# Two-pass inducing-point attention: the second pass three batches behind the first, with weights loaded in pieces

## The chip, the cores and the metric

One core of one Trainium2 chip runs the whole program. The metric is device time in microseconds (us), median over several executions; lower is better. The profile is of one execution; its span, from the first to the last recorded instruction, is about 2 us shorter than the time measured for the same execution (159.9 against 161.84 us for the kernel before).

Executions of this program differ by 1 to 3%, and the clock that is granted to the matmul engine differs between them. Runs are therefore marked fast or slow: a run of a single-core program counts as slow when it is over 1.5% above the fastest of its kernel.

Short names: PE is the matmul engine, DVE the vector engine, ACT the scalar (activation) engine, POOL the GpSimd engine. The names L148 and so on are lines of the kernel.

## The reference, cut to what matters

```python
# x: (4, 12480, 128) f32, inducing: (32, 128), w_in: (128, 2048), w_out: (2048, 128)
def mab(q, kv):
    s = scale * (q @ kv.transpose(0, 2, 1))
    a = np.exp(s - s.max(-1, keepdims=True))
    a /= a.sum(-1, keepdims=True) + 1e-09
    return a @ kv
h   = mab(I, x)        # 32 inducing points attend to all rows of a batch
att = mab(x, h)        # every row attends to the 32 points of its batch
g   = gelu(att @ w_in) # exact gelu
out = g @ w_out        # (49920, 128) f32
```

There are two passes over x. No row of a batch can enter the second pass before the whole batch has gone through the first, because `h` sums over all rows. The values are so small that the kernel takes the two-layer network on the 32 points instead of on every row: it works out q, 32 rows of 128, per batch, and the second pass averages rows of q. A check on the core tests the conditions of that shortcut and branches to a general version if they fail. They hold here.

## The kernel before: the parts that matter

A batch is cut into 7 units, 6 of 2048 rows and a tail of 192; there are 28 units in all. `s` is the step; a step does pieces of the first pass for the newest units and of the second pass for units that are LAG steps older:

```python
    LAG = n_u + 5                      # 12 units
    ...
        a0, a1, a2 = au(0), au(1), au(2)      # first pass: units s, s-1, s-2
        b0, b1 = bu(0), bu(1)                 # second pass: units s-LAG, s-LAG-1
        lone = a0 is None
        if a0: a_transpose(bat(a0), a0, 0)    # PE transposes x, DVE copies to xT
        if a1: a_score(bat(a1), a1)           # PE scores, ACT exponential e1t, POOL adds to acc
        if a0: load_next()                    # issues the DMA of a later unit of x
        pump()                                # one stage of precompute, if one is pending
        if b1:
            b_sum(bat(b1), b1)                # PE sums e2, DVE reciprocal
            b_out(bat(b1), b1, 0, False)      # PE matmul 'at', DVE scales it into o
            b_out(bat(b1), b1, 1, True)       # PE matmul 'at', ACT copies, POOL scales
        pump()
        if a0: a_transpose(bat(a0), a0, 1)
        if b0: b_score(bat(b0), b0)           # PE scores, ACT exponential e2 (2 buffers)
        pump()
        if b1:
            b_out(bat(b1), b1, 2, False)
            b_out(bat(b1), b1, 3, lone)       # the last one also issues the 1 MB output DMA
        pump()
        if a2:
            a_gather(bat(a2), a2)             # PE gathers e1t * x into hun
            if a2.tail: chains.append(precompute(bat(a2)))
```

`precompute` makes q of a batch after its tail: hT (the 32 points), pt = w_in applied to them (PE), slope and offs (DVE), then

```python
        nc.gpsimd.tensor_tensor(out=sl, in0=pt, in1=slope..., op=ALU.mult)      # POOL, 128x512
        nc.gpsimd.tensor_tensor(out=gl, in0=sl, in1=offs..., op=ALU.subtract)   # POOL, 128x512
        yield
        ... qp_ps += gl.T @ w_out_h  (16 matmuls on PE), then q
```

The loads of x come in as f16 into 9 buffers `xh`; an `xh` buffer comes free when its gather is done. Loads are issued from POOL's queue, outputs from SP's. The weights are loaded whole:

```python
    for _ in range(3): load_next()            # two were issued before: units 0 to 4
    nc.gpsimd.dma_start(out=w_in_h, in_=moe_w_in)
    nc.gpsimd.dma_start(out=w_out_h, in_=moe_w_out...)
    for _ in range(3): load_next()            # units 5 to 7
```

The order of instructions on an engine's queue is settled when the program is built, and it is not the order of the Python lines: in the trace below, PE does the scores of a unit ahead of the four `at` matmuls of an earlier one, two of which are written first. I call this the built order, and "in turn" the order of the lines.

Of the kernel before, what the change touches and what calls it, by code (L numbers as in the profile page):

```python
# [8 lines left out]
FP32 = mybir.dt.float32  # L9
FP16 = mybir.dt.float16  # L10
INT32 = mybir.dt.int32
AF = mybir.ActivationFunctionType
ALU = mybir.AluOpType
AX = mybir.AxisListType

B = 4
N = 12480
M = 32
C = 128
DFF = 2048  # L20
NBLK = DFF // 128
# [35 lines left out]
def kernel(  # L57
# [8 lines left out]
    nc = tc.nc  # L66
# [1 line left out]

    consts = ctx.enter_context(tc.tile_pool(name="consts", bufs=1))
    main = ExitStack()  # L70
    xt_pool = main.enter_context(tc.tile_pool(name="xt", bufs=3))
    sb = main.enter_context(tc.tile_pool(name="sb", bufs=2))
    pre = main.enter_context(tc.tile_pool(name="pre", bufs=2))
    ps = main.enter_context(tc.tile_pool(name="ps", bufs=1, space=PSUM))

    units = [[Unit(b, i) for i in range(NFULL + 1)] for b in range(B)]
# [24 lines left out]
    w_in_h = consts.tile([128, DFF], FP16)  # L101
    w_out_h = consts.tile([128, NBLK, 128], FP16)
# [3 lines left out]
    for j in range(4):  # L106
# [3 lines left out]
        out=stack4,  # L110
        in_=identity.rearrange("p (j m) -> p m j", j=4),
        axis=AX.X,
        op=ALU.add,
# [3 lines left out]
        out=same_m, in_=stack4.unsqueeze(1).broadcast_to([128, 4, M])  # L117
# [4 lines left out]
    n_u = NFULL + 1  # L122
# [4 lines left out]
    class Batch:  # L127
        def __init__(self, b):
            self.b = b
            self.rr2 = pre.tile([128, n_u, 4, 4], FP32, tag="rr2")  # L130
            nc.gpsimd.memset(self.rr2[:, NFULL, :, :], 1.0 / M)
            self.xT = xt_pool.tile([128, N], FP16, tag="xT", name=f"xT{b}")

            self.acc = pre.tile([128, 16, M], FP32, tag="acc")
            self.hun = ps.tile([128, C], FP32, tag="hun", name=f"hun{b}")
            self.live = {}

        def xT_of(self, u, c0, c1):
            return self.xT[:, u.t0 + c0 * u.p : u.t0 + c1 * u.p]
# [111 lines left out]
    def precompute(bt):  # L251
        hun_sb = pre.tile([128, C], FP32, tag="hun_sb")
        nc.scalar.activation(out=hun_sb, in_=bt.hun, func=AF.Copy)
        r1s = pre.tile([128, M], FP32, tag="r1s")
        nc.vector.tensor_reduce(
            out=r1s, in_=bt.acc.rearrange("p c m -> p m c"), axis=AX.X, op=ALU.add
        )
        yield
        h_ps = ps.tile([128, 2, M], FP32, tag="misc")
        nc.tensor.matmul(h_ps[:, 0, :], ones_f, r1s, start=True, stop=True)  # L260
        nc.tensor.matmul(h_ps[:, 1, :], hun_sb, stack4, start=True, stop=True)
        yield
        rr1 = pre.tile([128, M], FP32, tag="rr1")
        nc.vector.reciprocal(out=rr1, in_=h_ps[:, 0, :])
        in_range(rr1, 1.0 / R_HIGH, 1.0 / R1_LOW, bt.b, 0)
        bt.hT = pre.tile([128, M], FP16, tag="hT")
        nc.vector.tensor_tensor(out=bt.hT, in0=h_ps[:, 1, :], in1=rr1, op=ALU.mult)

        yield
        pt_ps = ps.tile([128, NBLK, M], FP32, tag="misc")  # L270
        for blk in range(NBLK):
            nc.tensor.matmul(
                pt_ps[:, blk, :],
                w_in_h[:, blk * 128 : (blk + 1) * 128],
                bt.hT,
                start=True,
                stop=True,
            )
        yield
        pt = pre.tile([128, NBLK, M], FP32, tag="pt")  # L280
        nc.scalar.activation(out=pt, in_=pt_ps, func=AF.Copy)
        hs = pre.tile([128, NBLK], FP32, tag="hs")
        nc.vector.tensor_reduce(out=hs, in_=pt, axis=AX.X, op=ALU.add)
        slope = pre.tile([128, NBLK], FP32, tag="slope")
        nc.vector.tensor_scalar(
            out=slope,
            in0=hs,
            scalar1=2.0 * CGELU / M,
            scalar2=0.5,
            op0=ALU.mult,  # L290
            op1=ALU.add,
        )
        offs = pre.tile([128, NBLK], FP32, tag="offs")
        nc.vector.scalar_tensor_tensor(
            out=offs,
            in0=hs,
            scalar=CGELU / (M * M),
            in1=hs,
            op0=ALU.mult,
            op1=ALU.mult,  # L300
        )
        sl = pre.tile([128, NBLK, M], FP32, tag="sl")
        nc.gpsimd.tensor_tensor(
            out=sl,
            in0=pt,
            in1=slope.unsqueeze(2).broadcast_to([128, NBLK, M]),
            op=ALU.mult,
        )
        gl = pre.tile([128, NBLK, M], FP16, tag="gl")
        nc.gpsimd.tensor_tensor(  # L310
            out=gl,
            in0=sl,
            in1=offs.unsqueeze(2).broadcast_to([128, NBLK, M]),
            op=ALU.subtract,
        )
        yield
        qp_ps = ps.tile([128, 128], FP32, tag="misc")
        for blk in range(NBLK):
            j = blk % 4
            nc.tensor.matmul(  # L320
                qp_ps[32 * j : 32 * j + 32, :],
                gl[:, blk, :],
                w_out_h[:, blk, :],
                start=(blk < 4),
                stop=(blk >= NBLK - 4),
            )
        yield
        qp = pre.tile([128, 128], FP32, tag="qp")
        nc.scalar.activation(out=qp, in_=qp_ps, func=AF.Copy)
        yield  # L330
        q_ps = ps.tile([128, 128], FP32, tag="misc")
        nc.tensor.matmul(q_ps, same_m.rearrange("p j m -> p (j m)"), qp, start=True, stop=True)
        bt.q = pre.tile([128, 4, 128], FP16, tag="q")
        nc.vector.tensor_tensor(  # L334
            out=bt.q,
            in0=q_ps.unsqueeze(1).broadcast_to([128, 4, 128]),
            in1=strand.unsqueeze(2).broadcast_to([128, 4, 128]),
            op=ALU.mult,
        )
        yield  # L340
        check_gelu(bt, pt, hs)
# [34 lines left out]
        o = sb.tile([128, 16, 128], FP32, tag="o", bufs=4)  # L376
        bt.live[("o", u.idx)] = o

    def b_out(bt, u, ci, on_act):
        if ci >= u.nci:  # L380
            return
        e2 = bt.live[("e2", u.idx)]
        o = bt.live[("o", u.idx)]
        rr2 = bt.rr2[:, u.idx, :, :]
        ov = o[:, : u.nc, :].rearrange("p (j ci) d -> p ci j d", ci=u.nci)
        at = ps.tile([128, 4, 128], FP32, tag="big", bufs=4)
        nc.tensor.matmul(  # L387
            at[: u.p, : u.nj, :],
            e2[: u.rows, ci * u.p : (ci + 1) * u.p],
            bt.q[: u.rows, : u.nj, :],  # L390
            start=True,
            stop=True,
        )
        dst = ov[: u.p, ci, :, :]
        by = rr2[: u.p, ci, : u.nj].unsqueeze(2).broadcast_to([u.p, u.nj, 128])
        if on_act:
            nc.scalar.activation(out=dst, in_=at[: u.p, : u.nj, :], func=AF.Copy)  # L397
            nc.gpsimd.tensor_tensor(out=dst, in0=dst, in1=by, op=ALU.mult)  # L398
        else:
            nc.vector.tensor_tensor(out=dst, in0=at[: u.p, : u.nj, :], in1=by, op=ALU.mult)  # L400
        if ci == u.nci - 1:
            base = u.b * N + u.t0
            nc.sync.dma_start(
                out=out[base : base + u.nc * u.p, :].rearrange(
                    "(p c) d -> p c d", p=u.p
                ),
                in_=o[: u.p, : u.nc, :],
            )

    order = [u for b in range(B) for u in units[b]]  # L410
# [2 lines left out]
    def load_next():  # L413
        nonlocal loaded
        if loaded < len(order):
            a_load(order[loaded])
            loaded += 1

    n_all = B * n_u

    LAG = n_u + 5
    batches = {}

    def at_step(s):
# [8 lines left out]
        def bat(u):  # L433
            if u.b not in batches:
                batches[u.b] = Batch(u.b)
            return batches[u.b]

        def pump():
            if chains:
                try:  # L440
                    next(chains[0])
                except StopIteration:
                    chains.pop(0)

        a0, a1, a2 = au(0), au(1), au(2)
        b0, b1 = bu(0), bu(1)
        lone = a0 is None
        if a0:
            a_transpose(bat(a0), a0, 0)
        if a1:  # L450
            a_score(bat(a1), a1)
        if a0:
            load_next()
        pump()
        if b1:
            b_sum(bat(b1), b1)
            b_out(bat(b1), b1, 0, False)
            b_out(bat(b1), b1, 1, True)
        pump()
        if a0:  # L460
            a_transpose(bat(a0), a0, 1)
# [1 line left out]
            b_score(bat(b0), b0)  # L463
        pump()
        if b1:
            b_out(bat(b1), b1, 2, False)
            b_out(bat(b1), b1, 3, lone)
        pump()
        if a2:
            a_gather(bat(a2), a2)  # L470
# [9 lines left out]
            )  # L480

    chains = []
    for _ in range(3):
        load_next()
    nc.gpsimd.dma_start(out=w_in_h, in_=moe_w_in)
    nc.gpsimd.dma_start(
        out=w_out_h, in_=moe_w_out.rearrange("(blk p) d -> p blk d", p=128)
    )
    for _ in range(3):
        load_next()  # L490
    for s in range(n_all + LAG + 1):
        at_step(s)

# [12 lines left out]
        out=failed,  # L506
        in0=tot,
# [177 lines left out]
```

## Time and profile before

| | before |
|---|---|
| time, four runs in all | 161.52 us median (160.19 to 162.86) |
| first and last output issued | 56.2 and 152.2 us |
| PE, POOL, DVE, ACT busy | 73%, 60%, 55%, 48% of the span |
| second pass alone at clock 0.5 | 3.39 us a unit |

(The profiled run took 161.84 us; it carries the slow mark, but it lies in the middle of the kernel's four runs.)

The slice rows of the page cut the span into 40 slices of 4 us. A digit is the busy share of a slice in tenths; PEclk is the granted clock of PE in tenths; GB/s is what the DMA engines moved. Of the kernel before:

```profile
PE   0379606987865999997699999599798568888400
...
PEclk9999955699998579999858999779999755556755
DMA  2999999999999899999999986506679835378991
GB/s 39 212 212 212 193 209 213 213 213 212 214 214 199 141 199 284 377 331 304 323 310 287 415 359 271 234 37 246 271 291 394 359 144 189 146 320 322 410 384 37
```

Two things are to be seen. Until about 50 us the DMA is full at 212 GB/s, counted in f16, with loads alone. And after 92 us the DMA is often not full although only outputs are left, which go at up to 410 GB/s in a slice. The Trainium skill ("Trainium Kernel Development and Optimization", Key Constraints) says that DMAs from all queues share the same 16 engines; the trace agrees, for from 60 to 92 us loads and outputs run together and the DMA row stays at 9.

The windows view gives busy time by stretch. Its columns are: from and to, length, busy us (and instructions) of PE, PEld, DVE, ACT and POOL, clock, DMA share, GB/s. Of the kernel before:

```profile
0.00:56.00 56.00, 35.98 (x664) 27.96 (x665) 17.95 (x45) 23.57 (x36) 31.75 (x51) 0.86 1.03 193
56.00:92.00 36.00, 33.12 (x501) 21.34 (x499) 30.67 (x73) 21.55 (x36) 23.04 (x31) 0.88 1.03 315
92.00:152.00 60.00, 47.41 (x489) 21.83 (x486) 40.06 (x113) 31.48 (x61) 40.46 (x46) 0.78 0.65 267
```

A share of 1.03 is to be read as full. The last stretch has a DMA share of 0.65 in 60 us: 60 x 0.35 = 21 us of empty DMA. The bytes to be moved are 13.8 MB in, 25.6 MB out, so empty DMA in the body of the program is the time that could be won.

Why the DMA runs empty there is in the chain of waits, followed back from the end; each line has start, length and what. Of the kernel before, one unit of second pass alone at clock 0.5:

```profile
134.53 0.61 ACT e_2539 L354
...
135.18 0.27 PE r_2549 L366 x4
135.46 0.55 PE s_2563 L346 x4
136.00 1.83 PE at L387 x4
...
137.92 0.61 ACT e_2568 L354
```

From one exponential to the next is 137.92 - 134.53 = 3.39 us. `at` of 136.00 belongs to the unit before e_2539. There are two e buffers, so the exponential e_2568 can only start when those four `at` matmuls have read the old buffer, and the sum of the next unit and the scores of the one after it go first.

### The profile page before, as it was taken

The page shows a single profiled execution, that of the slowest core. Times are in us where ns is not written, and L with a number is a line of the kernel's source. Part 1 is how long each engine was busy: PE and PEld are TensorE (multiplying, and loading weights), DVE is VectorE, ACT ScalarE, POOL GpSimd, SP SyncE. Part 2 cuts the span into 40 slices and gives each one's busy share as a digit, 9 for nine tenths or more (in the row PEclk, how much of TensorE's full clock was granted, in tenths as well). Part 3 has the DMA queues.
Part 4 walks back from the last instruction along what each step waited for, and adds up shares of the span by engine and source line. Part 5 has one row for each costly group of instructions (what it writes and reads, how often), then busy time and mean ns, then how long its engine had stood idle before and what let it go on. Part 6 is the DMA issues. An engine that isn't in the chain of part 4 may idle for free. (4 is left out here: it accounts for less than half of the span.)

```text
span 159.9 us, 4086 instructions
## 1 busy us (share of the span) xinstructions
PE 116.5 (73%) x1647; PEld 71.1 (44%) x1647; DVE 88.7 (55%) x229; ACT 76.6 (48%) x132; POOL 95.3 (60%) x127
## 2 busy tenths in 40 slices
PE   0379606987865999997699999599798568888400
PEld 0367406866753466666345757365323232223100
DVE  2223102223542998899859779588777772554700
ACT  3045601667373365684455667337666324446400
POOL 7823710564839963799673457835969950667900
PEclk9999955699998579999858999779999755556755
DMA  2999999999999899999999986506679835378991
GB/s 39 212 212 212 193 209 213 213 213 212 214 214 199 141 199 284 377 331 304 323 310 287 415 359 271 234 37 246 271 291 394 359 144 189 146 320 322 410 384 37
DMA packets 10087, 39.71 MB, mean 248 GB/s; under 512 B 2992, under 2 KB 3792, under 8 KB 6992
## 3 DMA queue, kind: packets, MB, share of 16 engines
q0 software_dynamic: 6112, 13.83, 46.3%
q1 hardware_dynamic: 3952, 25.58, 39.5%
q8 instruction: 14, 0.23, 0.5%
q14 instruction: 9, 0.07, 0.1%
HBM read 27.67 MB, written 25.56 MB: 333 GB/s over the span
## 5 line engine op out<-in xcount | busy, mean ns | idle before, releaser
L148 PE MATMUL tr<-identity_h,xh 128*128 128x128 f16 x392 | 36.3, 246 | 12.7 <-DMA xh<-in_x_dram 12.4
L148 PEld LDWEIGHTS <-xh 128*128 128x128 f16 x392 | 27.9, 111 | 21.2 <-DMA xh<-in_x_dram 14.3
L175 POOL TENSOR_TENSOR acc<-acc,e1t 128x512 f32<-128x512 f32 (+1 forms) x24 | 24.4, 1016 | 17.7 <-ACT e1t L168 15.5
L397 ACT ACTIVATE o<-at 128x512 f32<-128x512 f32 (+1 forms) x39 | 21.4, 562 | 12.6 <-PE at L387 8.1
L83 POOL DMA_DIRECT2D xh<-in_x_dram x28 | 15.9, 570 | 9.9 <-DMA xh<-in_x_dram 3.7
L398 POOL TENSOR_TENSOR o<-o,rr_1587 128x512 f32<-128x512 f32 (+1 forms) x13 | 12.5, 992 | 8.1 <-ACT o L397 8.1
L153 DVE COPY xT_118<-tr 128x1024 f16<-128x1024 f16 (+1 forms) x7 | 4.4, 629 | 19.1 <-PE tr L148 19.1
L155 ACT ACTIVATE xT_118<-tr 128x1024 f16<-128x1024 f16 x6 | 6.0, 1024 | 17.0 <-PE tr L148 17.0
L398 POOL TENSOR_TENSOR o<-o,rr_947 128x512 f32<-128x512 f32 (+1 forms) x12 | 11.7, 988 | 3.8 <-ACT o L397 2.3
L400 DVE TENSOR_TENSOR o<-at,rr_459 128x512 f32<-128x512 f32 (+1 forms) x19 | 11.9, 658 | 1.9 <-PE at L387 1.8
L400 DVE TENSOR_TENSOR o<-at,rr_116 128x512 f32<-128x512 f32 (+1 forms) x19 | 12.0, 658 | 0.3 <-PE at L387 0.2
L185 PEld LDWEIGHTS <-e1t 128*32 128x32 f16 x392 | 7.4, 98 | 6.7 <-issue 4.6
L153 DVE COPY xT_461<-tr 128x1024 f16<-128x1024 f16 (+1 forms) x7 | 4.4, 629 | 9.7 <-PE tr L148 9.7
L400 DVE TENSOR_TENSOR o<-at,rr_947 128x512 f32<-128x512 f32 (+1 forms) x14 | 8.8, 650 | 0.2
L155 ACT ACTIVATE xT_461<-tr 128x1024 f16<-128x1024 f16 x6 | 6.2, 1025 | 4.7 <-PE tr L148 4.7
L400 DVE TENSOR_TENSOR o<-at,rr_1587 128x512 f32<-128x512 f32 (+1 forms) x13 | 7.7, 639 | 0.0
L398 POOL TENSOR_TENSOR o<-o,rr_459 128x512 f32<-128x512 f32 (+1 forms) x7 | 6.6, 949 | 1.7 <-ACT o L397 1.7
L346 PEld LDWEIGHTS <-hT 128*32 128x32 f16 x100 | 4.0, 97 | 7.3 <-issue 6.1
L155 ACT ACTIVATE xT_949<-tr 128x1024 f16<-128x1024 f16 x6 | 6.2, 1027 | 1.9 <-PE tr L148 1.8
L155 ACT ACTIVATE xT_1589<-tr 128x1024 f16<-128x1024 f16 x6 | 6.2, 1025 | 1.8 <-PE tr L148 1.8
L398 POOL TENSOR_TENSOR o<-o,rr_116 128x512 f32<-128x512 f32 (+1 forms) x7 | 6.7, 953 | 0.1
L173 POOL CAST acc<-e1t 128x512 f32<-128x512 f16 x4 | 2.4, 610 | 6.9 <-ACT e1t L168 6.9
(349 smaller groups left out, 249.0 us busy)
## 6 DMA issues: line engine op xcount, KB each, us to landing
out_dram<-o SPq DMA_DIRECT2D x24, 1024.0 KB, 5.3
xh<-in_x_dram POOLq DMA_DIRECT2D x24, 512.0 KB, 10.3
w_in_h<-in_moe_w_in_dram POOLq DMA_DIRECT2D x1, 512.0 KB, 15.3
w_out_h<-in_moe_w_out_dram POOLq DMA_DIRECT2D x1, 512.0 KB, 17.5
out_dram<-o SPq DMA_DIRECT2D x4, 96.0 KB, 4.6
xh<-in_x_dram POOLq DMA_DIRECT2D x4, 48.0 KB, 9.1
ind_s<-in_inducing_dram SPq DMA_DIRECT2D x1, 16.0 KB, 1.6
```

The lines of the kernel that those rows point to most:

```text
L83: nc.gpsimd.dma_start(out=xh[: u.p, : u.nc, :], in_=src)
L148: nc.tensor.transpose(tr[:, c - c0, : u.p], xh[: u.p, c, :], identity_h[: u.p, : u.p])
L153: nc.vector.tensor_copy(out=dst, in_=tr[:, : c1 - c0, : u.p])
L155: nc.scalar.activation(out=dst, in_=tr[:, : c1 - c0, : u.p], func=AF.Copy)
L173: nc.gpsimd.tensor_copy(out=acc, in_=e1t)
L175: nc.gpsimd.tensor_tensor(out=acc, in0=acc, in1=e1t[: u.p, : u.nc, :], op=ALU.add)
L185: nc.tensor.matmul(bt.hun[32 * j : 32 * j + 32, :], e1t[: u.p, j * u.nci + ci, :], xh[: u.p, j * u.nci + ci, :], start=(u.idx == 0 and ci ...
L346: nc.tensor.matmul(s2[32 * j : 32 * j + 32, : u.cols], bt.hT, bt.xT_of(u, j * u.nci, (j + 1) * u.nci), start=True, stop=True,)
L397: nc.scalar.activation(out=dst, in_=at[: u.p, : u.nj, :], func=AF.Copy)
L398: nc.gpsimd.tensor_tensor(out=dst, in0=dst, in1=by, op=ALU.mult)
L400: nc.vector.tensor_tensor(out=dst, in0=at[: u.p, : u.nj, :], in1=by, op=ALU.mult)
```

## The change

Its intent, as I read it: give the first pass the DMA alone for three batches, so that q of a batch is ready long before it is wanted and the two passes disturb each other less. The second pass then trails by 21 units instead of 12. All four batches of transposed x stay resident. Two 128x512 operations of precompute move from POOL to DVE, and the weights come in four pieces between the loads of x. Attention with a block-diagonal q was there already; that part of the diff (a split of `b_out` into `b_diag` and `scaled`, left out here) leaves the work as it was, except that which of the scalings go to ACT and POOL differs a little: the fourth in every batch but the first.

```diff
-    xt_pool = main.enter_context(tc.tile_pool(name="xt", bufs=3))
+    xt_pool = main.enter_context(tc.tile_pool(name="xt", bufs=4))
-    pre = main.enter_context(tc.tile_pool(name="pre", bufs=2))
+    pre = main.enter_context(tc.tile_pool(name="pre", bufs=1))
... (rr2 and acc get bufs=2, hT and q bufs=B)
-        nc.gpsimd.tensor_tensor(            # sl, and the same for gl
+        nc.vector.tensor_tensor(
...
-    LAG = n_u + 5
+    LAG = 3 * n_u
...
         if a0:
             load_next()
+            if weight_loads and s % 2:
+                dst, src = weight_loads.pop(0)
+                nc.gpsimd.dma_start(out=dst, in_=src)
...
-    for _ in range(3):
+    for _ in range(7):
         load_next()
-    nc.gpsimd.dma_start(out=w_in_h, in_=moe_w_in)
-    nc.gpsimd.dma_start(out=w_out_h, in_=moe_w_out...)
-    for _ in range(3):
-        load_next()
+    weight_loads = [
+        (w_in_h[:, :half_f], moe_w_in[:, :half_f]),
+        (w_in_h[:, half_f:], moe_w_in[:, half_f:]),
+        (w_out_h[:, :half_b, :], w_out_src[:, :half_b, :]),
+        (w_out_h[:, half_b:, :], w_out_src[:, half_b:, :]),
+    ]
```

So the pieces of the weights are issued at steps 1, 3, 5 and 7, behind at least nine loads of x.

More of the change, by code (lines that the diff above doesn't have):

```diff
@@ L129, in __init__ @@
             self.b = b
-            self.rr2 = pre.tile([128, n_u, 4, 4], FP32, tag="rr2")
+            self.rr2 = pre.tile([128, n_u, 4, 4], FP32, tag="rr2", bufs=2)
             nc.gpsimd.memset(self.rr2[:, NFULL, :, :], 1.0 / M)
             self.xT = xt_pool.tile([128, N], FP16, tag="xT", name=f"xT{b}")
-            self.acc = pre.tile([128, 16, M], FP32, tag="acc")
+            self.acc = pre.tile([128, 16, M], FP32, tag="acc", bufs=2)
             self.hun = ps.tile([128, C], FP32, tag="hun", name=f"hun{b}")
@@ L265, in precompute @@
         in_range(rr1, 1.0 / R_HIGH, 1.0 / R1_LOW, bt.b, 0)
-        bt.hT = pre.tile([128, M], FP16, tag="hT")
+        bt.hT = pre.tile([128, M], FP16, tag="hT", bufs=B)
         nc.vector.tensor_tensor(out=bt.hT, in0=h_ps[:, 1, :], in1=rr1, op=ALU.mult)
@@ L309, in precompute @@
         gl = pre.tile([128, NBLK, M], FP16, tag="gl")
-        nc.gpsimd.tensor_tensor(
+        nc.vector.tensor_tensor(
             out=gl,
@@ L332, in precompute @@
         nc.tensor.matmul(q_ps, same_m.rearrange("p j m -> p (j m)"), qp, start=True, stop=True)
-        bt.q = pre.tile([128, 4, 128], FP16, tag="q")
+        bt.q = pre.tile([128, 4, 128], FP16, tag="q", bufs=B)
         nc.vector.tensor_tensor(
@@ L377, in b_sum, with scaled, b_diag @@
         bt.live[("o", u.idx)] = o
-    def b_out(bt, u, ci, on_act):
+    def scaled(dst, at, by, on_act):
+        if on_act:
+            nc.scalar.activation(out=dst, in_=at, func=AF.Copy)
+            nc.gpsimd.tensor_tensor(out=dst, in0=dst, in1=by, op=ALU.mult)
+        else:
+            nc.vector.tensor_tensor(out=dst, in0=at, in1=by, op=ALU.mult)
+    def b_diag(bt, u, ci, on_act):
         if ci >= u.nci:
@@ L383, in b_out @@
         o = bt.live[("o", u.idx)]
-        rr2 = bt.rr2[:, u.idx, :, :]
-        ov = o[:, : u.nc, :].rearrange("p (j ci) d -> p ci j d", ci=u.nci)
         at = ps.tile([128, 4, 128], FP32, tag="big", bufs=4)
@@ L393, in b_out @@
         )
-        dst = ov[: u.p, ci, :, :]
-        by = rr2[: u.p, ci, : u.nj].unsqueeze(2).broadcast_to([u.p, u.nj, 128])
-        if on_act:
-            nc.scalar.activation(out=dst, in_=at[: u.p, : u.nj, :], func=AF.Copy)
-            nc.gpsimd.tensor_tensor(out=dst, in0=dst, in1=by, op=ALU.mult)
-        else:
-            nc.vector.tensor_tensor(out=dst, in0=at[: u.p, : u.nj, :], in1=by, op=ALU.mult)
-        if ci == u.nci - 1:
+        scaled(
+            o[: u.p, : u.nc, :].rearrange("p (j ci) d -> p ci j d", ci=u.nci)[:, ci, :, :],
+            at[: u.p, : u.nj, :],
+            bt.rr2[: u.p, u.idx, ci, : u.nj].unsqueeze(2).broadcast_to([u.p, u.nj, 128]),
+            on_act,
+        )
+    def b_out(bt, u, part):
+        b_diag(bt, u, 2 * part, False)
+        b_diag(bt, u, 2 * part + 1, part == 0 or bt.b > 0)
+        if part == 1:
             base = u.b * N + u.t0
@@ L406, in b_out @@
                 ),
-                in_=o[: u.p, : u.nc, :],
+                in_=bt.live[("o", u.idx)][: u.p, : u.nc, :],
             )
@@ L446, in at_step @@
         b0, b1 = bu(0), bu(1)
-        lone = a0 is None
         if a0:
@@ L456, in at_step @@
             b_sum(bat(b1), b1)
-            b_out(bat(b1), b1, 0, False)
-            b_out(bat(b1), b1, 1, True)
+            b_out(bat(b1), b1, 0)
         pump()
@@ L465, in at_step @@
         if b1:
-            b_out(bat(b1), b1, 2, False)
-            b_out(bat(b1), b1, 3, lone)
+            b_out(bat(b1), b1, 1)
         pump()
@@ L482 @@
     chains = []
-    for _ in range(3):
+    for _ in range(7):
         load_next()
-    nc.gpsimd.dma_start(out=w_in_h, in_=moe_w_in)
-    nc.gpsimd.dma_start(
-        out=w_out_h, in_=moe_w_out.rearrange("(blk p) d -> p blk d", p=128)
-    )
-    for _ in range(3):
-        load_next()
+    w_out_src = moe_w_out.rearrange("(blk p) d -> p blk d", p=128)
+    half_f, half_b = DFF // 2, NBLK // 2
+    weight_loads = [
[4 more added lines that the diff above has]
+    ]
     for s in range(n_all + LAG + 1):
```

## The prediction

> **What bounds the kernel now.** The slice rows show DMA 90% or more busy at 212 GB/s for the first 50 us: only x arrives (as f16; 13.8 MB with the weights, about 65 us at that rate). Output goes at up to 426 GB/s (two-microsecond windows): 25.6 MB need about 60 us. Both share the DMA engines, as the Trainium skill says ("Trainium Kernel Development and Optimization", Key Constraints); the trace agrees: from 60 to 92 us both run and the DMA stays full. The DMA floor is about 3 (start) + 65 + 2 (weights go slowly, 168 GB/s at 18-20 us) + 60 + 3 (end) = 133 us; 161 are taken. The rest is lost after 92 us, where windows show mean DMA shares of 0.3 to 0.8: over 20 us of empty DMA. A step with both passes takes 3.6 to 3.9 us there; the last units, second pass alone, take 3.39 us each (chain of waits) against 2.46 us of DMA: the clock is 0.5, and the exponential of unit u+2 waits for the at matmuls of unit u (ACT idle 1.81 us, two e buffers), because the last q came only at 130 us.
>
> **What the change does.** No work is removed. The lag grows from 12 to 21 units, so first-pass steps, bound by DMA (2.47 us a unit), stay alone for 21 units, and q is ready 14 units before its use, which removes the wait for q (51, 126-131 us). Mixed steps fall from about 16 to 7; second-pass-only units grow from about one and a half batches to three. sl and gl go from POOL (2 x 1.04 us) to DVE (2 x 0.67 us, an estimate from o of the same shape). Weights in pieces remove PE's 6.5 us wait at 18-25 us, but no DMA work: under 1 us.
>
> **Sum.** Unit 21 lands at about 58 us; first output about 62 us (now 56.2). Seven mixed steps at 3.6 us, to about 85 us; reads and writes (8.5 + 15 us) fill the DMA. Then 18 full units and 3 tails of the second pass alone. At clock 1.0 the old trace has three such units at 2.35 to 2.85 us (115 to 123 us), with ACT 1.8, POOL 2.1, DVE 1.6 us of work each, so the DMA (2.46 us) about binds. At clock 0.5 PE needs about 2.8 us. I take 2.6 on average: 47 us, tails 3, the last precompute 2, landing and end 6: 142 us.
>
> **Prediction: 142 us, 136 to 150.** Faster by over 2%: 0.92; within 2%: 0.06; slower: 0.02.
>
> **What would show it.** First output near 62 us; DMA full at 212 GB/s until then; afterwards 330 to 426 GB/s to the end, without the holes of 92-152 us; no PE wait over 1 us for q; second-pass-only units at 2.4 to 2.8 us; POOL near 80% busy there.
>
> **What would make it wrong.** The granted clock: if PE stays at 0.5 through the second pass and the late order of the at matmuls returns, units take 3.4 us and the time is about 156. The skill ("TensorE: Matmul & The Clock Gate", Part 1) says that activity releases the throttle; here 132-147 us stayed at 0.5 with PE 83% busy, so I don't count on it. Or POOL, 2.1 us a unit, delays the output buffers; or precompute stalls PE in the first pass beyond what nine x buffers hide.

## The result, and the profile after

The changed kernel takes 173.3 us (172.64 to 174.11, four runs), against 161.52 us. The ratio is 1.076, with a 95% interval of 1.066 to 1.086. A ratio here is the mean time of one kernel's fast runs over that of the other's fast runs of the same rounds, so it is not quite the ratio of the medians. The prediction was 142 us, and faster: wrong in size and in direction. The clock does not explain it: the profiled run of after has a mean clock of 0.823, that of before 0.82. All outputs are right.

The slice rows of the kernel after (slices of 4.3 us):

```profile
PE   0489857469859885199997697965886787779500
...
PEclk9999996965978999656999879997869789555855
DMA  3999999999999899910555069765791989678892
GB/s 51 211 215 213 212 212 200 209 209 187 192 208 183 139 194 216 207 20 25 226 246 226 23 276 395 319 288 223 332 398 67 397 370 430 269 309 334 372 422 77
```

The plateau at 212 GB/s is longer, as intended. But then come two slices with 20 and 25 GB/s: around 73 to 81 us the DMA has almost nothing to do, and after that it stays at half. The loads are over (the last unit of x landed at 74.5 us), and outputs have not begun.

The output transfers as the tile view lists them (count, duration of the issue in ns, first and last start), the kernel before, then after:

```profile
L403 SPq DMA_DIRECT2D out_dram<-o x28: 332/332/659, 56.2 to 152.2; - x28
```

```profile
L413 SPq DMA_DIRECT2D out_dram<-o x28: 332/332/544, 80.1 to 163.5; - x28
```

The outputs start 23.9 us later and then take 83.4 us instead of 96.0, which gives back 12.6. That leaves 11.3 us, close to the 10.8 us by which the span grew. Windows of the kernel after, cut at the end of the loads and at the start of the steps with second pass alone:

```profile
0.00:72.00 72.00, 48.16 (x957) 39.20 (x961) 30.59 (x68) 31.30 (x45) 40.12 (x63) 0.89 1.03 192
72.00:105.00 33.00, 29.12 (x436) 18.16 (x434) 24.33 (x64) 17.73 (x33) 16.27 (x21) 0.83 0.42 168
105.00:163.00 58.00, 43.14 (x264) 14.63 (x262) 36.61 (x100) 31.04 (x61) 39.70 (x43) 0.78 0.78 321
```

The second pass alone does run with less empty DMA, 58 x 0.22 = 12.8 us. But the stretch of mixed steps before it, which used to be full, now has 33 x 0.58 = 19.1 us of empty DMA. Together 31.9 us, against 21.0 us before: the difference is the loss. What was one hole in the old kernel was made smaller, and a larger one was opened ahead of it.

The first pass does not keep up with the loads. The table has, for three units, when x landed and when the exponential of its first pass began (us), from the traces:

| unit | before | after |
|---|---|---|
| 12 | 40.2, then 48.1 | 36.5, then 52.6 |
| 16 | 47.8, then 67.7 | 48.8, then 60.6 |
| 20 | 56.5, then 84.5 | 57.9, then 74.8 |

In the kernel before, units 16 and 20 wait in steps that also bring outputs; up to unit 12 it has first-pass work alone, and there it trails by 8 us. The kernel after has first-pass work alone up to unit 20, and trails by 12 to 17 us.

The PE timeline of the kernel after shows one reason; in brackets is the idle time just before the line and what ended it:

```profile
48.80 1.09 PE L149 MATMUL tr<-identity_h,xh 128*128 128x128 f16 x10 [2.17 <-DMA xh<-in_x_dram]
49.83 0.62 PE L186 MATMUL hun_466<-xh,e1t 128*32 128x128 f16 x16
50.38 0.61 PE L161 MATMUL s_878<-indT,xT_464 128*128 128x32 f16 x16
```

PE stood still for 2.17 us until unit 16's x landed, while the scores of unit 12 (s_878), whose x had landed 12 us before and whose last copy into xT ended at 41.5 us, stood behind that transpose in the queue. The Trainium skill ("TensorE: Matmul & The Clock Gate", Part 3) says that matmuls keep their order strictly and only weight loads are pulled ahead; the trace agrees.

A second reason is precompute, which now runs into its own new costs. The timeline of the kernel after, DVE and POOL and then PE, for the second batch:

```profile
66.63 0.68 DVE L304 TENSOR_TENSOR sl<-pt,slope 128x512 f32<-128x512 f32 x1
...
67.35 4.49 DVE L311 TENSOR_TENSOR gl<-sl,offs 128x512 f16<-128x512 f32 x1
67.48 1.16 POOL L176 TENSOR_TENSOR acc<-acc,e1t 128x512 f32<-128x512 f32 x1
...
69.13 1.05 POOL L213 TENSOR_TENSOR zsq<-pt 128x512 f32<-128x512 f32 x1
70.14 1.15 POOL L176 TENSOR_TENSOR acc<-acc,e1t 128x512 f32<-128x512 f32 x1
...
71.90 0.62 PE L321 MATMUL qp_ps<-w_out_h,gl 128*32 128x128 f16 x16 [4.30 <-DVE gl L311]
```

`gl` took 4.49 us on DVE while POOL did three operations of its own, and PE waited 4.30 us for it. The tile view of the four `gl` (min, median, max in ns), before on POOL and then after on DVE:

```profile
L310 POOL TENSOR_TENSOR gl<-sl,offs x4: 1037/1048/1059, 48.8 to 126.1; 128x512 f16<-128x512 f32 x4
```

```profile
L311 DVE TENSOR_TENSOR gl<-sl,offs x4: 674/1658/4492, 51.3 to 115.8; 128x512 f16<-128x512 f32 x4
```

The Trainium skill ("SBUF — State Buffer", Who interferes with whom) says that a DVE instruction with two inputs in SBUF contends with a GpSimd instruction that reads SBUF, by an exclusive lock. The trace agrees: 0.67 us undisturbed, 4.49 us beside POOL. Of the 4.49 us, 0.13 lie before the first of the three POOL operations and 0.55 after the last (71.29 us), which together is the undisturbed time: it is as if `gl` had stood still in between, although by the records it had started first. Whether it costs time is a question for the experiments.

In the part with the second pass alone, the chain of waits of the kernel after has a shorter loop at full clock:

```profile
128.00 0.61 ACT e_2353 L355
...
128.65 0.27 PE r_2363 L367 x4
...
129.12 0.64 DVE o L385
...
129.80 0.59 PE at L394 x2
130.39 0.39 PE at L394
...
130.87 0.61 ACT e_2382 L355
```

From 128.00 to 130.87 is 2.87 us, still through the two e buffers and the late `at`, and not through the DMA (2.46 us for an output of 1 MB at 426 GB/s). At clock 0.5 it is 3.39 us, as before.

### The profile page after: what moved, and what is told of

Its sections match the earlier page's. It is cut to its first block, busy times and chain, and to the rows that moved or that the text cites. A ratio compares the mean times of both kernels' runs of the same rounds, so it can differ in the third digit from the quotient of the medians.

```text
span 170.7 us, 4088 instructions
## 1 busy us (share of the span) xinstructions
PE 120.4 (71%) x1647; PEld 72.0 (42%) x1647; DVE 91.5 (54%) x230; ACT 80.1 (47%) x139; POOL 96.5 (57%) x128
## 3 DMA queue, kind: packets, MB, share of 16 engines
q0 software_dynamic: 6272, 13.83, 43.8%
HBM read 27.67 MB, written 25.56 MB: 312 GB/s over the span
## 5 line engine op out<-in xcount | busy, mean ns | idle before, releaser
L149 PE MATMUL tr<-identity_h,xh 128*128 128x128 f16 x392 | 37.8, 251 | 14.7 <-DMA xh<-in_x_dram 13.2
L149 PEld LDWEIGHTS <-xh 128*128 128x128 f16 x392 | 28.6, 113 | 19.5 <-DMA xh<-in_x_dram 16.4
L83 POOL DMA_DIRECT2D xh<-in_x_dram x28 | 15.6, 561 | 30.0 <-PE hun_120 L186 18.1
L382 ACT ACTIVATE o<-at 128x512 f32<-128x512 f32 (+1 forms) x46 | 24.8, 567 | 7.9 <-PE at L394 4.6
L383 POOL TENSOR_TENSOR o<-o,rr_916 128x512 f32<-128x512 f32 (+1 forms) x13 | 12.6, 989 | 7.0 <-ACT o L382 7.0
L383 POOL TENSOR_TENSOR o<-o,rr_1365 128x512 f32<-128x512 f32 (+1 forms) x13 | 12.5, 989 | 6.0 <-ACT o L382 6.0
L383 POOL TENSOR_TENSOR o<-o,rr_462 128x512 f32<-128x512 f32 (+1 forms) x13 | 13.1, 1027 | 4.5 <-ACT o L382 2.7
L385 DVE TENSOR_TENSOR o<-at,rr_116 128x512 f32<-128x512 f32 (+1 forms) x19 | 12.2, 657 | 1.9 <-PE at L394 1.7
L154 DVE COPY xT_464<-tr 128x1024 f16<-128x1024 f16 (+1 forms) x7 | 4.4, 630 | 14.6 <-PE tr L149 14.6
L383 POOL TENSOR_TENSOR o<-o,rr_116 128x512 f32<-128x512 f32 (+1 forms) x7 | 6.6, 949 | 9.0 <-ACT o L382 8.6
L186 PEld LDWEIGHTS <-e1t 128*32 128x32 f16 x392 | 8.3, 104 | 7.5 <-issue 3.9
L154 DVE COPY xT_118<-tr 128x1024 f16<-128x1024 f16 (+1 forms) x7 | 4.4, 630 | 13.1 <-PE tr L149 13.1
L311 DVE TENSOR_TENSOR gl<-sl,offs 128x512 f16<-128x512 f32 x4 | 8.5, 2120 | 0.1
L154 DVE COPY xT_918<-tr 128x1024 f16<-128x1024 f16 (+1 forms) x7 | 4.4, 628 | 7.7 <-PE tr L149 7.7
L385 DVE TENSOR_TENSOR o<-at,rr_462 128x512 f32<-128x512 f32 (+1 forms) x13 | 8.2, 644 | 0.1
L385 DVE TENSOR_TENSOR o<-at,rr_1365 128x512 f32<-128x512 f32 (+1 forms) x13 | 7.7, 639 | 0.0
L385 DVE TENSOR_TENSOR o<-at,rr_916 128x512 f32<-128x512 f32 (+1 forms) x13 | 7.6, 631 | 0.0
```

The source lines that it names most:

```text
L83: nc.gpsimd.dma_start(out=xh[: u.p, : u.nc, :], in_=src)
L149: nc.tensor.transpose(tr[:, c - c0, : u.p], xh[: u.p, c, :], identity_h[: u.p, : u.p])
L154: nc.vector.tensor_copy(out=dst, in_=tr[:, : c1 - c0, : u.p])
L186: nc.tensor.matmul(bt.hun[32 * j : 32 * j + 32, :], e1t[: u.p, j * u.nci + ci, :], xh[: u.p, j * u.nci + ci, :], start=(u.idx == 0 and ci ...
L311: nc.vector.tensor_tensor(out=gl, in0=sl, in1=offs.unsqueeze(2).broadcast_to([128, NBLK, M]), op=ALU.subtract,)
L382: nc.scalar.activation(out=dst, in_=at, func=AF.Copy)
```

## The experiments

Theory L, at first: the long lag itself costs the time, because loads and outputs no longer overlap; the later expectations call this theory O (overlap). Rivals: G, the contention of `gl` on DVE; W, the weights that come late in pieces; the built order of PE's queue, which spoils the first pass (T) or the second (C). Later, K: the granted clock in the second pass alone.

Two kinds of result have to be kept apart. Any edit makes the build lay out all queues anew, so a kernel with one edit undone also has another order. That is why the later runs hold the order.

### One part undone at a time

**a1_gl_on_pool**: after, with `sl` and `gl` back on POOL.

```diff
-        nc.vector.tensor_tensor(out=sl / gl, ...
+        nc.gpsimd.tensor_tensor(out=sl / gl, ...
```

> The kernel after, with sl and gl back on POOL. Theory G (gl on DVE, which took up to 4.49 us beside POOL and held PE for 4.30 us at 67.6-71.9 us): no PE wait over 2 us for gl, first output near 75 us instead of 80.1, time 166 to 168 us. Rival L (the long lag itself, which puts the whole second pass behind the reads): first output stays at 78-80 us and the time at 171 us or more, because PE is behind for other reasons.

Measured: 174.22 us (173.28 to 175.56), ratio to before 1.080 (1.071 to 1.088); first output at 78.4 us, last at 165.5. Theory G falls as the cause. PE still waits for `gl`, now made on POOL, but 3.1 us in all and 2.3 at the longest, where after has 5.9 and 4.3; the time did not fall.

**a2_lag_alone**: before, with only the lag and the buffers that it forces.

```diff
-    LAG = n_u + 5
+    LAG = 3 * n_u      # and the buffer counts of the change
```

> The kernel before with the lag of 21 units and only the buffers that this forces (four xT, hT and q, single small temporaries); gl on POOL, weights whole. Theory L: 169 us or more, first output after 74 us, second pass 28 units in about 83 us. Rival G: the lag alone gives 160 us or less, since what hurts is gl on DVE. Rival W (weights in pieces slow the reads): 165 us or less.

Measured: 169.22 us (166.89 to 170.33), before 161.61 us in the same rounds; two of its four runs have the slow mark, so no ratio was given. First output at 75.4 us, last at 158.7 (profile of a fast run). The two fast runs (168.12 and 166.89) lie 6 us above the mean of before (161.3), so the lag alone, in the order that the build gives it, makes about half of the loss; it stays below the 169 us that theory L expected.

**a3_weights_whole**: after, with the weights loaded whole as before.

```diff
-    for _ in range(7):
+    for _ in range(3):
+        load_next()
+    nc.gpsimd.dma_start(out=w_in_h, in_=moe_w_in)
+    nc.gpsimd.dma_start(out=w_out_h, in_=moe_w_out...)
+    for _ in range(3):
         load_next()      # and no weight_loads in the steps
```

> The kernel after, with the weights loaded as before in two whole transfers behind the first five units. Theory W: reads end at 69-70 us instead of 73 and the time falls by 3 us or more. Theories L and G: within 2 us of 173, since the second pass starts when PE gets to it and not when the reads end; the early wait of PE for x at 18-25 us comes back.

Measured: 168.0 us (166.27 to 169.28), ratio 1.036 (1.026 to 1.045). The first output came at 73.4 us instead of 80.1. By the ratios of fast runs that is 6.5 us better than after (1.076 - 1.036 of 161 us), where theories L and G expected 2 at most. But the loads ended at 72.5 us, not at 69 to 70 (after: 74.5), so theory W was right in size and not in its reason. And in this run the wait for `gl` was also shorter, 1.50 us at the place where after has 4.30, so the gain is not shown to be the weights' alone. Run d1 below tells what the weights cost with the order held.

**a4_order_forced**: after, with the second pass held in turn on PE (scores and sums behind the last `at`).

```diff
-        nc.tensor.matmul(at...
+        last_at[0] = nc.tensor.matmul(at...
...
-            b_score(bat(b0), b0)
+            with tc.issue_after(last_at[0].ins):
+                b_score(bat(b0), b0)      # and b_sum likewise
```

> The kernel after, with PE's queue held to the order sums, two at matmuls, scores of the next unit, two at matmuls. Theory C (the built order puts the at matmuls of unit u behind the scores of unit u+2, and with two e buffers exponential and at matmuls then take turns: 2.86 us a unit at clock 1.0, 3.39 at 0.5): second-pass-only units take 2.4 to 2.6 us, time 163 to 167 us, DMA share over 0.9 from 110 us on. Rival P (POOL, 2.1 us a unit, or the granted clock sets the pace): units stay at 2.9 us or more and the time within 3 us of 173.

Measured: 170.94 us (167.49 to 173.83), no ratio (two slow runs). A miss. The second pass alone still took 58.7 us (101.4 to 160.1), against 58.4 in after. Its units at clock 0.5 did fall from 3.39 to 3.1 us, but this run had about 38 us at clock 0.5 there, after about 26. Both times the total was the same; this raised theory K.

### The order held

The next kernels put every group of PE work behind the one that is written before it:

```python
    @contextmanager
    def in_turn():
        if last_pe[0] is None:
            yield
        else:
            with tc.issue_after(last_pe[0]):
                yield
        mine = [i for i in nc.cur_bb.bb.instructions if i.engine == mybir.EngineType.PE]
        last_pe[0] = mine[-1]
```

**b1_first_pass_in_turn** and **b2_all_in_turn**: after, with `a_transpose`, `a_score` and `a_gather` in turn; b2 also `b_score`, `b_sum` and `b_out`.

```diff
-            a_score(bat(a1), a1)
+            with in_turn():
+                a_score(bat(a1), a1)      # and so for the other parts
```

> The kernel after, with PE's queue held to the written order for the first pass only (transposes of unit s, scores of s-1, gather of s-2). Theory T (the built order runs the transposes three to five units ahead of the scores and gathers, PE takes its queue in order, so each score waits for x that lands 10 to 16 us later, and the second pass, queued behind, starts that much late): the first exponential of a unit follows its landing by about 5 us instead of 10 to 16, first output at 66 to 70 us instead of 80.1, time 162 to 167 us. Rival M (mixed steps and precompute hold it, not the order): first output stays after 76 us.

Measured for b1: 170.7 us (169.81 to 171.4), ratio 1.065 (1.053 to 1.077). First output at 77.1 us, not at 66 to 70: a miss. In its trace PE now waits 4.39 us at 48.6 us for a piece of `w_out`, and 2.53 and 2.43 us for `gl`.

> The kernel after, with PE's queue held to the written order for both passes. If T and C both hold: first output at 66 to 70 us, second-pass-only units at 2.5 us with clock 1.0 and about 3.0 with 0.5, time 155 to 162 us. If only the overlap of the two passes counts (theory O: a mixed step costs 3.6 us, the two parts apart 2.5 + 2.9), it stays above 161.6, the kernel before.

Measured for b2: 166.57 us (165.36 to 167.65), ratio 1.039 (1.025 to 1.052); outputs from 77.1 to 158.1. So with the order of the lines after is 6 us faster than with the order of the build (1.076 - 1.039 of 161 us), and still slower than before, as theory O expected; the first output missed the 66 to 70 us of theories T and C. PE's timeline of b2 shows a wait that is left:

```profile
42.34 0.29 PE L321 MATMUL qp_ps<-w_out_h,gl 128*32 128x128 f16 x8
48.41 0.40 PE L321 MATMUL qp_ps<-w_out_h,gl 128*32 128x128 f16 x8 [5.78 <-DMA w_out_h<-in_moe_w_out_dram]
```

The first half of `w_out` was there, the second was issued at 34.4 us and landed at 48.4, and everything behind it in PE's queue stood for 5.78 us.

**b3_before_in_turn**: the kernel before, all in turn.

> The kernel before (lag 12) with the same order of PE's queue held. Theory O: better than b2, 150 to 157 us, since the second pass starts at about 50 us and most of it runs beside the reads. If the built order was good for the short lag, within 2 us of 161.6 or slower.

Measured: 155.55 us (155.36 to 156.6), ratio 0.973 (0.962 to 0.983). Order is worth 2.7% to the old kernel too. So order is not what the change broke; it is a cost that both have.

**b4_after_lag12**: after, with the lag of before and nothing else.

```diff
-    LAG = 3 * n_u
+    LAG = n_u + 5
```

> The kernel after with the lag of 12 units; all other parts of the change stay (gl on DVE, weights in pieces, nine units loaded first). If the lag is the cause (L): 160 to 166 us. If the parts other than the lag cost about 5 us, as a3 says of the weights: 165 to 167.

Measured: 159.96 us (159.76 to 160.15), ratio 0.998 (0.989 to 1.008); outputs from 56.5 to 150.8. With the short lag the rest of the change costs or gains at most about 1%. With the long one in the built order it is 12.5 us slower (1.076 - 0.998).

### The lag in turn

**c1_lag21_in_turn**, **c2_lag17_in_turn**, **c3_lag14_in_turn**: b3 with the buffers of the change, and weights and `gl` as before. The three differ in one number.

```diff
-    LAG = n_u + 5
+    LAG = 3 * n_u        # c1: 21;  c2: 2 * n_u + 3;  c3: 2 * n_u
```

> The kernel before with PE's queue in the written order (as in b3) and the lag of 21 units, weights whole, gl on POOL. So only the lag differs from b3. Theory O (a long lag loses the overlap: the second pass starts when the reads end, and its own pace stays above the 2.46 us that the DMA needs): first output at 68 to 72 us, pass of 82 us, time 158 to 163 us, so slower than b3 (155.6). Rival T alone (only the bad order made the long lag slow): 150 us or less.

> As c1 with a lag of 17 units. Theory O: between b3 and c1, 156 to 160 us, first output near 62 us.

> As c1 with a lag of 14 units. Theory O with the wait for q counted: q of a batch is ready at 49 us, so two units more of lag cost little of the start and remove the wait; 153 to 157 us. If no wait for q is left to remove, 157 or more.

| kernel | lag | median us (range) | ratio to before (95%) | outputs from, to |
|---|---|---|---|---|
| b3 | 12 | 155.55 (155.36 to 156.6) | 0.973 (0.962 to 0.983) | 53.0, 146.2 |
| c3 | 14 | 154.57 (153.06 to 156.33) | 0.959 (0.952 to 0.966) | 54.0, 147.4 |
| c2 | 17 | 159.53 (158.78 to 160.51) | 0.992 (0.985 to 0.999) | 66.4, 151.3 |
| c1 | 21 | 163.37 (160.69 to 164.48) | 1.005 (0.996 to 1.014) | 70.8, 154.6 |

(The profiles of c1 and c3, from which the last column comes, are of slow runs, 164.48 and 156.33 us; the ratios are of fast ones. Two of c1's four runs are slow. c2's first output was expected near 62 us and came at 66.4. b3 has 3 buffers of xT and 2 of each precompute tile, the others those of the change.) From lag 14 to 21 the cost is 1.005 - 0.959 of 161 us, 7.5 us, with the code, order and buffers otherwise the same. From lag 12 to 21 (b3 to c1) it is 5.2 us. Between 12 and 14 the intervals overlap, so which of the two is better is not shown. c3 is faster than both kernels.

Windows of c3 (the slow run), cut at its first output and after its loads:

```profile
0.00:54.00 54.00, 35.96 (x726) 29.21 (x726) 19.97 (x47) 26.37 (x39) 33.49 (x55) 0.94 1.05 198
54.00:93.00 39.00, 32.28 (x564) 21.32 (x564) 33.40 (x83) 22.32 (x39) 26.82 (x32) 0.96 1.01 318
93.00:147.00 54.00, 43.37 (x359) 16.66 (x358) 35.04 (x99) 28.80 (x56) 35.78 (x42) 0.67 0.69 286
```

The middle stretch, loads and outputs together, is full again (1.01 in 39 us, where after had 0.42 in 33 us). What is empty is 54 x 0.31 = 16.7 us at the end, less than before's 21.0.

In c2, the steps just after the last load, at clock 1.0, show what a unit costs without the late `at` (ACT, the exponentials; what is left of the first pass, gathers and the last tail, still runs beside them):

```profile
98.96 0.60 ACT L354 ACTIVATE e<-s 128x512 f16<-128x512 f32 x1
...
100.99 0.59 ACT L354 ACTIVATE e<-s 128x512 f16<-128x512 f32 x1
...
103.16 0.59 ACT L354 ACTIVATE e<-s 128x512 f16<-128x512 f32 x1
```

That is 2.0 to 2.2 us a unit, less than the DMA needs. With the second pass truly alone, run d1 below shows it: five outputs from 117.1 to 128.9 us, 2.36 us each, at clock 1.0. Its window:

```profile
117.00:129.00 12.00, 7.81 (x53) 2.35 (x53) 7.78 (x19) 7.65 (x16) 10.14 (x11) 1.00 0.91 384
```

So the prediction's "the DMA about binds" is right for the order of the lines (a share of 0.91), and was wrong for the order that the build made (2.87 us). At clock 0.5 c2 mostly takes 3.0 to 3.1 us a unit, as a4 did; the held order brings it down from 3.39 and no further.

### The weights, and the clock

**d1_pieces_earlier**: b2, with the four pieces issued at steps 0 to 3.

```diff
-            if weight_loads and s % 2:
+            if weight_loads:
```

> b2 with the four weight pieces issued at steps 0 to 3 instead of 1, 3, 5, 7. Theory W2 (what the pieces cost at the long lag is the last piece's late landing, 48.4 us, for which PE's queue stands still for 5.78 us): that wait is gone or below 1 us, first output 3 to 6 us earlier than 77.1, time 161 to 164 us instead of 166.6. Rival: the cost is the reads themselves (DMA share of the pieces) or gl on DVE, and the time stays within 1.5 us of 166.6.

Measured: 161.18 us (159.39 to 162.47), ratio 1.006 (0.998 to 1.013). That is 5.3 us better than b2. The last piece landed at 40.9 us, and the sixteen matmuls now run without the wait, as PE's timeline of d1 has it:

```profile
44.49 0.41 PE L321 MATMUL qp_ps<-w_out_h,gl 128*32 128x128 f16 x16
```

Theory W is confirmed with the order held: late weights cost 5 us. And d1 (pieces, `gl` on DVE) equals c1 (whole, `gl` on POOL): once the weights are in time, neither of these parts of the change matters. Windows of d1, a fast run of 159.39 us:

```profile
0.00:71.00 71.00, 50.62 (x1028) 41.18 (x1029) 31.87 (x81) 35.10 (x52) 43.74 (x69) 0.90 1.04 197
71.00:93.00 22.00, 19.72 (x360) 12.08 (x361) 19.70 (x54) 14.64 (x27) 13.51 (x15) 1.00 0.62 257
93.00:149.00 56.00, 40.22 (x261) 12.01 (x259) 36.37 (x97) 30.58 (x62) 40.02 (x44) 0.82 0.80 331
```

The empty DMA is now 22 x 0.38 + 56 x 0.20 = 19.6 us, against 31.9 in after. But the first output still comes at 72.1 us, when the loads are just over (71.3 us): not one output overlaps a load. From there on at least 60 us of outputs are left, and the mixed steps after 71 us leave PE busy 90% of the time at full clock while the DMA has 0.62.

**c4_at_twice**: b3, with each `at` done twice in the steps with second pass alone, to keep PE so busy that its clock stays up.

```diff
-        nc.tensor.matmul(at...
+        for _ in range(2 if lone_now[0] else 1):
+            nc.tensor.matmul(at...
```

> b3 with each at matmul of the second-pass-only steps run twice into the same PSUM bank (same result, about 1.7 us more PE work a unit at clock 0.5, 0.9 at 1.0). Theory K (the clock at 0.5 in 124-141 and 144-156 us holds the last units at 3.1 us): PE busy enough to be granted 1.0, those units at 2.6 us or less, time 151 to 155. Rival: the clock matters little there, or the doubled work only adds: units at 3.2 us or more, time 156 to 162.

Measured: 157.79 us (157.59 to 158.0), ratio 0.982 (0.978 to 0.986), no faster than b3 (0.973; the intervals overlap). From 133 to 148 us the clock was 1.0 and four outputs took 10.1 us (2.5 us a unit), but by then the double work had lost 3 us (the output of unit 21 was issued at 134.9 us, in b3 at 131.7). A miss.

**d2_lag14_twice_last**: c3, with the double `at` for the last batch only.

```diff
+        for _ in range(2 if u.b == B - 1 else 1):
```

> c3 (lag 14, written order) with each at matmul of the last batch alone run twice into the same bank. Theory K (the clock at 0.5 from 118 us on sets the 3.1 us of a unit there, and more PE work brings it to 1.0): the units of the last batch take 2.5 us, clock 1.0 from about 128 us, time 150 to 153 us. Rival (the doubled work at clock 0.5 costs as much as the clock gives back): 154 us or more.

Measured: 154.66 us (154.54 to 155.49), ratio 0.964 (0.957 to 0.970): the same as c3. The clock, though, was another; the stretch from 118 to 147 us in c3 (profile of a slow run) and in d2:

```profile
118.00:147.00 29.00, 22.72 (x114) 6.59 (x114) 14.73 (x44) 12.89 (x26) 19.29 (x23) 0.50 0.75 314
```

```profile
118.00:147.00 29.00, 21.75 (x140) 8.28 (x140) 14.76 (x44) 12.78 (x26) 19.01 (x21) 0.87 0.79 329
```

With more work the clock was 0.87 instead of 0.50, and the added work used it up: PE is busy about as long as before, and the DMA share moves from 0.75 to 0.79 only. (The fast runs agree: the mean clock of the whole run was 0.84 to 0.86 in c3 and 0.89 to 0.91 in d2.) Theory K falls as a lever: the clock is a real part of why the second pass alone is slow (2.36 us a unit at clock 1.0 in d1, 3.0 to 3.1 at 0.5 in c2), but this way of raising it gains nothing.

## Why the prediction was wrong

Its terms, against what the profiled run of after shows. Its parts add up to 143 us, which it gave as 142.

| term of the prediction | predicted | measured | difference |
|---|---|---|---|
| first output | 62 (unit 21 lands at 58) | 80.1 (unit 21 lands at 60.5) | +18.1 |
| seven mixed steps | 23 | 25.0 (80.1 to 105.1) | +2.0 |
| second pass alone, with tails and last precompute | 47 + 3 + 2 = 52 | 58.4 (105.1 to 163.5) | +6.4 |
| end of the last output, and time over span | 6 | 7.2 + 2.2 | +3.4 |

143 + 29.9 = 172.9, the time of that run.

- **The step that failed: "Unit 21 lands at about 58 us; first output about 62 us".** The landing was 2.5 us off. From landing to the first output I took 4 us; it was 19.6 us. I had read the first pass as "bound by DMA (2.47 us a unit)" and thus let PE keep pace with the loads for 21 units. It did not: unit 20's exponential began 17 us after its x had landed. The runs split a part of this. The order of the build put ready scores behind transposes that waited for x; holding it brought the first output from 80.1 to 77.1 us (b2). The late `w_out` held PE's queue; mending it brought 77.1 to 72.1 us (d1). What is left, 72.1 against 62, no run splits. In d1 unit 20 still began 9 us after its landing; PE was busy 17.5 of the 21 us from 51 to 72, at a mean clock of 0.84, with the precompute of the second batch among its work. And the sum had the wrong unit: in the order of the lines the first output belongs to step 22, which begins with the transposes of unit 22, and that landed at 61.2 us. The prediction had named "precompute stalls PE in the first pass beyond what nine x buffers hide" among what could make it wrong, and gave all of it too small a chance.
- **"Mixed steps fall ... reads and writes fill the DMA" failed with it.** Because of the late start, the loads were over before the first output. There was no unit whose load could share the DMA with an output; windows show a share of 0.42 where it had been full before. Steps that do both passes took 4.0 us in before, with the DMA full (nine outputs from 56.2 to 92.3 us), and 3.6 in after, with no load left to share it, against 2.47 + 2.87 apart, so a mixed step does both in less time. Cutting such steps from about 16 to 7 was counted as a gain, and was a loss.
- **"Weights in pieces ... under 1 us" was mis-sized, and in sign.** The wait early on was removed as said, but the last piece arrived at 48 us and at the long lag cost 5.3 us (b2 against d1, with the order held); with the lag of 12 such a cost does not show (b4).
- **"I take 2.6 on average" for a unit alone was mis-sized.** It was 2.87 us at clock 1.0 and 3.39 at 0.5. I had put the late `at` down to q coming late, and expected it to go away. It was in the built order all along: after has q early and the late `at` still. In the order of the lines the units do take 2.36 us at full clock (d1).
- **`sl` and `gl` on DVE at 0.67 us, an estimate from `o`, was off:** 0.67 to 4.49 us. `o` reads one input from PSUM, `gl` both from SBUF, and `gl` was slowed beside POOL, so `o` was the wrong thing to estimate from. It did not decide the time (a1).
- **Right:** the length of the plateau at 212 GB/s, the landing of unit 21, no wait for a late q in the second pass, and that the clock would not stay up in the second pass alone.

With ratios to before, in the terms of 161 us, the road from after to the best version is: 1.076 (after), to 1.039 with PE's order held (b2, 6 us), to 1.006 with the weights in time (d1, 5.3 us), and from 1.005 (c1, the same time as d1) to 0.959 with the lag at 14 (c3, 7.5 us). For the loss itself the same ratios give another sum, since before has the lag of 12 and a built order that costs it something too: 5.2 us for the lag from 12 to 21 with its buffers (b3 to c1), 5.3 for the late weights with `gl` on DVE (c1 to b2), and 6 for the built order of after (b2 to after) less the 4.4 that it costs before (b3). That is 12.2 us, the 7.6% of the result. So lag and late weights weigh about the same, and the weights cost it only together with the long lag: with the lag of 12 alone put back, in the built order, 12.5 us are gone (b4).

Open: which part of a3's 6.5 us is weights and which is the shorter wait for `gl` that came with its other order; why the clock is granted as it is in the second pass alone; whether b3 and c3 differ at all, and if so by the lag of 12 and 14 or by their buffers; and what holds the first output at 72 us in d1.

## What to carry to other kernels

When two phases load and store through the same DMA engines, the lag between them should be as short as the dependence allows with a little slack (here 12 to 14 units, where the dependence is one batch of 7): here every unit of lag beyond that took stores out of the time in which loads could share it, and was paid back at the end, about 1 us a unit from 14 to 21. "Bound by DMA" in a profile holds for the stretch in which it was read; before a phase is stretched, check for its last unit how far the compute trails behind the landing. And read the order of the engine's queue from the trace, not from the code: both kernels here gained 3 to 4% from being held to the order in which they are written.

## What the Trainium skill lacked or had wrong

- "TensorE: Matmul & The Clock Gate", Part 1, says that activity releases the throttle, and over what time it is watched, but not how large a share of that time must be busy. Here PE was busy by the records for 22.72 of 29 us at a clock of 0.50 throughout (c3, a slow run), and for 21.75 of 29 us at a mean of 0.87 with 140 instead of 114 matmuls (d2). Busy time alone does not tell which it will be.
- "DMA: Bandwidth & Descriptors", Where 436 GB/s comes from, says that for transfers between HBM and SBUF the HBM side binds, at about 358 GB/s, although the table of the page has one transfer at 425, for a core alone. Here a core worked alone too, and its stores reached 430 GB/s over a whole slice of 4.3 us (after) and 410 GB/s over one of 4.0 us (before): of the page's two figures the table's fits, and the section's sentence does not.
- The same page says that a load that casts has to be issued from GpSimd, but I found no rate for one there. Loads from f32 to f16 kept the DMA full at 212 GB/s, counted in f16. The source is f32, twice the bytes (the page of the profile has 27.67 MB read from HBM, where 13.83 MB are counted for the queue of the loads), so counted at the source this is 424 GB/s, about the pace of the outputs: a load of 1 MB of f32 took 2.47 us although it arrived as half of that, an output of 1 MB 2.46.
- "SBUF — State Buffer", Who interferes with whom, has the contention of `gl` right. It gives no size for such a case: 0.67 us became 4.49 us, over three GpSimd operations in a row. And it says that issue order decides who blocks; here `gl` was the one that waited, though by the records it started 0.13 us before the first of the three (times on POOL are rough).
- No page that I looked up warns that the built order of a queue can differ from the written one, or what it costs: 2.7% (before) and 3.7% of 161 us (after).
